# Stores of x moved to GpSimd, loads of a batch spread over its steps, first transposes a step later

## The chip, the cores and the metric

The kernel runs on one core of one Trainium2 chip. The metric is the device time of one execution in microseconds (us). The engines are named as in the profile: PE (TensorE) does matmuls and transposes, DVE (VectorE), ACT (ScalarE) and POOL (GpSimd) work on tiles, and SP (SyncE) issues most of the transfers; POOL and ACT can issue transfers of their own. Each engine works through its own instructions in order and waits on semaphores of the others.

## What is computed

Windowed attention, then a mixture of experts that takes one expert for each token, then a dense layer with softplus. All in float32, with 4 batches, 8 heads, 576 positions and 64 features to a head, so 2304 tokens of 512 features.

```python
def _attn_ref(q, k, v):                      # (4, 8, 576, 64) each
    rel = pos[:, None] - pos[None, :]
    mask_plain = (rel >= 0) & (rel < 32)                        # heads 0 to 3
    mask_dil = (rel >= 0) & (rel < 128) & (rel % 4 == 0)        # heads 4 to 7
    scores = np.where(masks, scale * (q @ k.T), -1e9)
    attn = np.exp(scores - scores.max(-1)); attn /= attn.sum(-1) + 1e-09
    return attn @ v
def _moe_ref(x, w_gate, w_output_gate, w1, w2):                 # x: (2304, 512), 8 experts
    e_idx = argmax(x @ w_gate)
    out[mask] = gate_w * eom[:, e] * (relu(x[mask] @ w1[e]) @ w2[e])
def _moe2_ref(x, w_in, w_out):               # (512, 2048), (2048, 512)
    h = x @ w_in
    return (np.maximum(h, 0.0) + np.log1p(np.exp(-np.abs(h)))) @ w_out
```

## The kernel before

Attention works on 20 tiles, five to a batch; tiles w = 0 to 3 of a batch hold 128 positions, tile w = 4 holds 64. Heads 0 to 3 (the "first half") use the plain window, heads 4 to 7 (the "second half") the dilated one. The main loop runs over steps i = 0 to 21 and is pipelined over tiles: step i computes the scores and the softmax's start of tile i (`scores` L346, L359; `softmax`, L373, L374; `exps` L382), transposes the probabilities of tile i - 1, multiplies them with v and normalises (`transpose_p` L388, `evict_p` L397, `sums` L423 to L427, `values` L415, `normalise` L437), and transposes x of tile i - 2 for the router (`transpose_x` L454, L465). A step is written out in that order, and each engine keeps it.

q and k come from DRAM as tiles `raw` (L261, `load_qk`; six buffers in rotation, each half of a batch needs two) and must be transposed before use: `transpose_qk` (L306, L314) makes one unit on PE, whose result `pqk` is evicted into `qT` and `kT` by ACT (L286, L290) or DVE (L288). A batch has ten units. They are done during the steps of the batch before; how many in each of its five steps is a small table, `QK_AT` for the later batches and `QK_0` for batch 1, whose transposes run in steps 0 to 4. v comes into `vP` (first half, L270, four transfers to a batch) and `vD` (second half, L275 and L279, two transfers to each of four heads), each kept twice, for even and odd batches. The unused parts of these tiles are cleared by POOL (`fills`, L235 to L243).

`normalise` writes the result x of a tile (five buffers) and stores it to `x_dram` through SP: the first 256 columns in one transfer (L444), the other 256 in four (L447), because the rows of the dilated half lie in another order in the tile. `x_dram` is read by the experts' gathers (L806), on POOL, through a list of tokens that POOL scatters into `idx_dram` (L600), one indirect transfer to a tile, in groups of tiles (0 to 3, 4 to 7, 8 to 10, 11 to 13, 14 to 16, 17 to 19).

All transfers of SP stand in one queue in the order in which the program writes them, and a transfer that waits holds all behind it. Beside the wait for its data or its buffer, each waits for the transfer eight places before it (eight lanes). POOL's transfers have eight lanes of their own. The expert stage and the last layer follow and are not touched.

Of the kernel before, what the change touches and what calls it, by code (L numbers as in the profile page):

```python
# [14 lines left out]
I32 = mybir.dt.int32  # L15
# [6 lines left out]
P = 128  # L22
# [18 lines left out]
def attn_moe_softplus_kernel(ctx: ExitStack, tc: tile.TileContext, q, k, v, w_gate, w_ogate, w1, w2, w_in, w_out, out, dbg=None):  # L41
    nc = tc.nc
    B, H, S, D = q.shape
# [6 lines left out]
    NW = 5  # L50
    NTL = B * NW
# [3 lines left out]
    G_PICK, G_DRAM = 2, 3  # L55
    GROUPS = [(0, 4), (4, 8), (8, 11), (11, 14), (14, 17), (17, 20)]

    const = ctx.enter_context(tc.tile_pool(name="const", bufs=1))
    dram = ctx.enter_context(tc.tile_pool(name="dram", bufs=1, space=DRAM))

    x_dram = dram.tile([NT, DM], F32, name="x_dram")
# [17 lines left out]
    first = const.tile([P, NE], F32, name="first")  # L79
    e0nt = const.tile([P, 1], F32, name="e0nt")  # L80
    tabp = const.tile([1, 1], I32, name="tabp")

    tl = {}

# [36 lines left out]
    def consts2():  # L121
        nc.gpsimd.memset(upper, 1.0)
        nc.gpsimd.affine_select(upper, upper, [[1, P]], ALU.is_gt, 0.0, base=0, channel_multiplier=-1)
        nc.gpsimd.memset(ones, 1.0)
        nc.gpsimd.memset(lg, 0.0)
        nc.gpsimd.memset(cumb, 0.0)
        nc.gpsimd.iota(rev, [[-1, NE]], base=NE, channel_multiplier=0, allow_small_or_imprecise_dtypes=True)
        nc.gpsimd.iota(eidx, [[1, NE]], base=0, channel_multiplier=0, allow_small_or_imprecise_dtypes=True)

        nc.gpsimd.memset(ebase, 0.0)  # L130
        nc.gpsimd.tensor_scalar(ebase[0:1], eidx[0:1], float(NT), None, ALU.mult)
        for b in range(B):
            nc.gpsimd.iota(pair[:, NW * b : NW * b + NW, 0], [[P, NW]], base=b * S, channel_multiplier=1)
# [121 lines left out]
    def load_qk(b, half):  # L255

        for ti, t in enumerate((q, k)):
            r = raw_p.tile([P, 2, 9 * D], F32, tag="raw", name=f"raw{b}{half}{ti}")
            raw[b, half, ti] = r
            src = t[b, 4 * half : 4 * half + 4].rearrange("(y x) (p j) d -> (x p) y (j d)", x=2, j=9)  # L260
            nc.sync.dma_start(r, src)  # L261

    def load_v(b, half):
        i = b % 2
        for h in range(4):
            h2, hp = h // 2, h % 2
            r = slice(64 * h2, 64 * h2 + 64)
            s = v[b, 4 * half + h]
            if half == 0:
                nc.sync.dma_start(  # L270
                    vP[i][r, hp, :, h2],
                    bass.AP(s.tensor, s.offset, [[D, 64], [32 * D, 17], [1, D]]),
                )
            else:
                nc.sync.dma_start(  # L275
                    vD[i][r, hp, 0:3, h2],
                    bass.AP(s.tensor, s.offset, [[4 * D, 64], [32 * 4 * D, 3], [1, 4 * D]]),
                )
                nc.sync.dma_start(  # L279
                    vD[i][64 * h2 : 64 * h2 + 48, hp, 3, h2],  # L280
                    s[4 * 96 :].rearrange("(m r) d -> m (r d)", r=4),
                )
# [44 lines left out]
    def pump(times=None):  # L327
        for e in bg[: PUMP[1]]:
            if e[1] > 0:
                e[1] -= 1  # L330
                continue
            for _ in range(PUMP[0] if times is None else times):
                e[1] = next(e[0], None)
                if e[1] is None:
                    bg.remove(e)
                if e[1] != 0:
                    break
# [81 lines left out]
    def sums(b, w):  # L419
# [7 lines left out]
        nc.vector.reciprocal(rc.rearrange("q a h c -> q a c h"), sm.rearrange("q (a c) h -> q a c h", a=2))  # L427
        pump()

    def normalise(b, w):  # L430
        d = tl[b, w]
        x = at_p.tile([P, 2, 4, D], F32, tag="x", name=f"x{b}{w}", bufs=5)
        d["x"] = x
        x2 = x.rearrange("q a h d -> q (a h d)")
        t0 = b * S + P * w
        nt = P if w < 4 else 64
        nc.vector.tensor_tensor(  # L437
            x,
            d["o"].rearrange("q a h c e -> q a (h c) e"),
            d["rc"].rearrange("q a h c -> q a (h c)").unsqueeze(3).to_broadcast([P, 2, 4, D]),  # L440
            ALU.mult,
        )
        pump()
        nc.sync.dma_start(x_dram[t0 : t0 + nt, :256], x2[:nt, :256])  # L444
        rows = x_dram[t0 : t0 + nt, 256:].rearrange("(m r) d -> m r d", r=4)
        for r in range(4):
            nc.sync.dma_start(rows[:, r], x2[32 * r : 32 * r + nt // 4, 256:])  # L447

    def transpose_x(b, w):
        d = tl[b, w]  # L450
# [557 lines left out]
    def hi_(r, j):  # L1008
        piece_hi(r, j)
# [24 lines left out]
    n = len(tiles)  # L1034
    todo, routes = [], []

    def some_qk(k):
        for _ in range(k):
            if todo:
                transpose_qk(*todo.pop(0))  # L1040

    QK_AT = [2, 2, 2, 2, 2]
    QK_0 = [0, 1, 3, 3, 3]

    EV = {}

# [21 lines left out]
    def events(i, s):  # L1068
        for what, *a in EV.get((i, s), ()):
            if what == "r":  # L1070
                bg.append([group(*a), 0, *a])
            elif what == "pl":
                logits_of(*a)
            elif what == "h":
                hi_(0, *a)
            elif what == "q":
                lo_(0, *a)
            elif what == "sc":
                diag_gathered(*a)
            elif what == "az":  # L1080
                acc0(*a)
            elif what == "mg":
                mm_gathered(a)
            elif what == "ll":
                load_late(*a)
            elif what == "go":

                e = next((e for e in bg if e[2] == a[0]), None)
                for _ in range(a[1]):
                    if e in bg:  # L1090
                        e[1] = next(e[0], None)
                        if e[1] is None:
                            bg.remove(e)
            elif what == "sl":
                g = next(g for g, (t0, t1) in enumerate(GROUPS) if t0 <= a[0] < t1)
                while any(e[2] == g for e in bg):
                    pump()
                sel_late(*a)
                split_late(*a)

    for i in range(n + 2):
        nqk = 0
        PUMP[0], PUMP[1] = (2, 1) if i < 12 else (4, 2) if i < n else (2, 2)
        if i == n - 5:
            rawx.close()
            K["wr"] = rctx.enter_context(tc.tile_pool(name="wr", bufs=RB, side="right"))
        if i == n - 4:
            per0x.close()
            K["w1"] = rctx.enter_context(tc.tile_pool(name="w1", bufs=4, side="right"))
            pctx = ExitStack()  # L1110
            for nm, bufs in (("xge", 4), ("sp0", 4), ("xl0", 5), ("sel", 4), ("rt2", 2)):
                K[nm] = pctx.enter_context(tc.tile_pool(name=nm, bufs=bufs, side="right"))
            K["slots"] = K["sel"].tile([P, CAPS[0]], F32, name="slots", bufs=1)
            nc.gpsimd.iota(K["slots"], [[1, CAPS[0]]], base=0, channel_multiplier=0, allow_small_or_imprecise_dtypes=True)
        if i < n:
            b, w = tiles[i]
            if b + 1 < B:
                nqk = (QK_AT if b else QK_0)[w]
                if w == 0:
                    if b == 0:  # L1120
                        fills(1)
                    todo += [(b + 1, *u_) for u_ in QK_UNITS]
                if w == 2:
                    for half in range(2):
                        load_v(b + 1, half)
                if w in (1, 3) and b + 2 < B:
                    load_qk(b + 2, w // 2)
            scores(b, w)
            softmax(b, w)
        if 1 <= i < n + 1:  # L1130
            transpose_p(*tiles[i - 1])
            evict_p(*tiles[i - 1])
        events(i, 0)
        some_qk(nqk - 1)
        if i < n:
            exps(*tiles[i])
        if 2 <= i:
            transpose_x(*tiles[i - 2])
            evict_x(i - 2)
            pump()  # L1140
        events(i, 1)
        if 1 <= i < n + 1:
            sums(*tiles[i - 1])
        events(i, 2)
        some_qk(min(nqk, 1))
        if 1 <= i < n + 1:
            values(*tiles[i - 1])
            normalise(*tiles[i - 1])
        events(i, 3)
        pump()  # L1150
        events(i, 4)
        pump()
        if i == n - 4:
            nc.vector.tensor_scalar(K["slots"], K["slots"], e0nt, None, ALU.add)
            K["rt"] = K["rt2"]
# [68 lines left out]
    x2, last_rank = {}, {}  # L1224
# [41 lines left out]
    for r in range(NE):  # L1266
        n = CAPS[r]
# [7 lines left out]
        for u in range(16):  # L1275
# [16 lines left out]
            if r + 1 < NE:  # L1292
                m = CAPS[r + 1]
# [6 lines left out]
            if r < NE - 1 or u < 8:  # L1300
                k_ = (r, 4 + u // 2) if u < 8 else (r + 1, (u - 8) // 2)
# [114 lines left out]
    for i in range(len(steps) + LAG):  # L1416
        if i < len(steps):
            b, f = steps[i]
# [52 lines left out]
```

## Time and profile before

| | us |
|---|---|
| median of 3 runs | 831.95 (831.78 to 834.63) |
| the profiled execution | 839.03 |
| its span in the profile | 837.5 |
| PE busy | 784.0 |
| DVE busy | 551.9 |
| ACT busy | 473.7 |
| POOL busy | 199.7 |

The granted clock of PE was 0.981 of full speed over the span. The page of the profile gives the totals, the span in 40 slices and the costliest lines. For a change inside attention three further views are of use: the waits, by engine, with the line that waits, who released it, the total, how often and the longest; the timeline, with the idle time before an instruction and its releaser in brackets; and the busy time of all engines in chosen stretches, with the granted clock and the DMA share. Times count from the start of the span.

### The profile page before, as it was taken

To read this page: it belongs to the slowest core of one execution; us is meant where nothing else is said; L and a number is where in the kernel's file an instruction comes from. 1 tells how busy PE (TensorE), PEld (TensorE's weight loads), DVE (VectorE), ACT (ScalarE), POOL (GpSimd) and SP (SyncE) were. 2 spreads that over 40 slices of the span, in tenths; PEclk is the share of its full clock that TensorE was granted. 3 is DMA by queue.
4 is the path that set the end of the run, shared out by engine and by line. 5 is a ranking of instruction groups with operands and counts; after the bars stand their busy time and mean duration, and the time that the engine had idled before them with its cause. 6 is when DMAs were issued, how large, how long until landed. Compare 5 with 4: busy or idle time off the path is not lost.

```text
span 837.5 us, 14769 instructions
## 1 busy us (share of the span) xinstructions
PE 784.0 (94%) x5542; PEld 701.9 (84%) x5543; DVE 551.9 (66%) x1079; ACT 473.7 (57%) x912; POOL 199.7 (24%) x173
## 2 busy tenths in 40 slices
PE   6788877799999999999899999999999999999995
PEld 5566645599999999999898878899999999999994
DVE  5467757474366776743778989886656665666653
ACT  3575633354546556655667566665655655655553
POOL 9501032435242454543202121211001001001001
PEclk9899989899999999999999999999999999999998
DMA  9979755418779889777832222221001001001000
GB/s 205 260 172 173 140 142 157 132 27 251 229 240 282 291 267 299 229 221 210 273 107 66 87 81 64 76 76 38 20 1 38 1 1 38 1 0 39 1 1 38
DMA packets 88844, 104.17 MB, mean 124 GB/s; under 512 B 31004, under 2 KB 65180, under 8 KB 88768
## 3 DMA queue, kind: packets, MB, share of 16 engines
q1 hardware_dynamic: 78688, 87.50, 38.3%
q0 software_dynamic: 3888, 10.12, 3.6%
q10 hardware_dynamic: 6192, 5.56, 2.0%
q8 instruction: 45, 0.74, 0.4%
q14 instruction: 31, 0.25, 0.1%
HBM read 83.98 MB, written 19.32 MB: 123 GB/s over the span
## 4 chain that ended last, share of the span: by engine, by line
PE 46%; issue 16%; DVE 6%; ACT 3%; POOL 1%; DMA 1%; SPq 0%; POOLq 0%; DVEq 0%
PE q L1380 4%; PE pg L840 4%; PE pg L841 4%; PE pg L839 4%; PE q L1378 4%; PE q L1379 4%; PE ph L839 3%; PE ph L841 3%; PE ph L840 3%; PE py L839 3%; PE py L840 3%; PE py L841 3%; DVE l L1358 1%; DVE gl L701 1%; ACT gh L1364 1%
## 5 line engine op out<-in xcount | busy, mean ns | idle before, releaser
L701 POOL TENSOR_TENSOR wl<-wr,wh 128x1024 fp32r<-128x1024 f32 (+1 forms) x46 | 99.5, 2170 | 204.0 <-ACT wh L785 108.3
L840 PE MATMUL pg<-xlm,wh 128*128 128x384 f32 x384 | 129.6, 338 | 0.0
L839 PE MATMUL pg<-xhm,wh 128*128 128x384 f32 x384 | 129.4, 337 | 0.0
L841 PE MATMUL pg<-xhm,wl 128*128 128x384 f32 x384 | 129.4, 337 | 0.0
L1380 PE MATMUL q<-wh,gl 128*128 128x512 f32 x288 | 114.0, 396 | 2.2 <-DVE gl L701 2.1
L1378 PE MATMUL q<-wh,gh 128*128 128x512 f32 x288 | 113.9, 396 | 0.4
L1379 PE MATMUL q<-wl,gh 128*128 128x512 f32 x288 | 113.1, 393 | 0.0
L1364 ACT CAST gh<-l 128x384 fp32r<-128x384 f32 x96 | 49.2, 512 | 99.9 <-DVE l L1358 99.9
L756 ACT CAST wh<-wr 128x1024 fp32r<-128x1024 f32 x72 | 75.2, 1049 | 16.2 <-ACT y L862 7.3
L701 DVE TENSOR_TENSOR gl<-l,gh 128x384 fp32r<-128x384 f32 x96 | 57.1, 595 | 41.0 <-ACT gh L1364 38.1
L839 PE MATMUL ph<-xh,wh 128*128 128x424 f32 (+7 forms) x256 | 80.7, 315 | 3.1 <-DVE hl L853 2.4
L1387 POOL DMA_INDIRECT out_dram<-o,perm_sb x18 | 18.6, 1035 | 271.9 <-DVE o L251 137.5
L839 PE MATMUL py<-hh,wh 128*128 128x424 f32 (+7 forms) x256 | 81.8, 320 | 0.0
L840 PE MATMUL py<-hl,wh 128*128 128x424 f32 (+7 forms) x256 | 80.7, 315 | 0.8 <-DVE hl L853 0.8
L841 PE MATMUL py<-hh,wl 128*128 128x424 f32 (+7 forms) x256 | 80.5, 314 | 0.0
L841 PE MATMUL ph<-xh,wl 128*128 128x424 f32 (+7 forms) x256 | 80.3, 314 | 0.0
L840 PE MATMUL ph<-xl,wh 128*128 128x424 f32 (+7 forms) x256 | 80.2, 313 | 0.0
L839 PEld LDWEIGHTS pg<-xhm,wh 128*128 128x128 f32 x384 | 72.1, 188 | 3.9
L701 DVE TENSOR_TENSOR wl<-wr,wh 128x1024 fp32r<-128x1024 f32 x42 | 61.9, 1478 | 20.4 <-ACT wh L756 14.1
L840 PEld LDWEIGHTS pg<-xlm,wh 128*128 128x128 f32 x384 | 72.1, 188 | 3.9
L841 PEld LDWEIGHTS pg<-xhm,wl 128*128 128x128 f32 x384 | 72.1, 188 | 0.0
L1349 DVE TENSOR_SCALAR w<-u 128x384 f32<-128x384 f32 x96 | 34.7, 362 | 56.4 <-ACT u L1347 55.6
(193 smaller groups left out, 1656.0 us busy)
## 6 DMA issues: line engine op xcount, KB each, us to landing
wr<-in_moe_w_dram SPq DMA_DIRECT2D x64, 512.0 KB
raw<-in_q_dram SPq DMA_DIRECT2D x8, 576.0 KB
raw<-in_k_dram SPq DMA_DIRECT2D x8, 576.0 KB
x2r<-yT_dram SPq DMA_DIRECT2D x12, 384.0 KB
vP<-in_v_dram SPq DMA_DIRECT2D x16, 272.0 KB
praw<-in_moe_w_in_dram SPq DMA_DIRECT2D x8, 512.0 KB
praw<-in_moe_w_out_dram SPq DMA_DIRECT2D x8, 512.0 KB
wr<-in_moe_w_in_dram SPq DMA_DIRECT2D x8, 512.0 KB
```

The costliest lines, as they stand in the source:

```text
L701: e.tensor_tensor(lo, src, hi.bitcast(F32), ALU.subtract)
L756: (eng or nc.scalar.copy)(d[1], d[0])
L839: nc.tensor.matmul(ps, wh, xh, start=(first and i == 0), stop=False)
L840: nc.tensor.matmul(ps, wh, xl, start=False, stop=False)
L841: nc.tensor.matmul(ps, wl, xh, start=False, stop=(last and i == k - 1))
L1349: nc.vector.tensor_scalar(w_, u, 1.0, None, ALU.add)
L1358: nc.vector.tensor_tensor(l, l, u, ALU.subtract)
L1364: nc.scalar.copy(gT[b, f][0], l)
L1378: nc.tensor.matmul(acc[b, t], gh[:, ts_], wh, start=(f == 0), stop=False)
L1379: nc.tensor.matmul(acc[b, t], gh[:, ts_], wl, start=False, stop=False)
L1380: nc.tensor.matmul(acc[b, t], gl[:, ts_], wh, start=False, stop=(f == NF - 1))
L1387: sc = nc.gpsimd.indirect_dma_start(out=out, out_offset=IndirectOffsetOnAxis(ap=perm_sb[:, b * (BT // P) + t, 0:1], axis=0), in_=o, in_off ...
```

## The change

Three things change, all in attention. x of tiles 0 to 13 (the first four routing groups) is stored by POOL: the first 256 columns directly, the other 256 by one indirect store with a table of row numbers, `xrow`, which four iotas fill at the start. Tiles w = 4 (numbers 4 and 9 among these) keep four small stores of their second half on SP. Tiles 14 to 19 keep the old way. The stores are declared independent of each other. Second, the loads for the next batches are emitted at the end of a step, behind `normalise`, and v of the next batch is split over steps w = 0, 2 and 4. Third, `QK_0` puts the first unit of batch 1 one step later.

```diff
+    xrow = const.tile([P, NTL], I32, name="xrow")
...
+        for r in range(4):
+            nc.gpsimd.iota(
+                xrow[32 * r : 32 * r + 32].rearrange("p (b w) -> p b w", w=NW),
+                [[2 * S, B], [2 * P, NW]], base=2 * r + 1, channel_multiplier=8,
+            )
...
-    def load_v(b, half):
+    def load_v(b, half, heads=range(4)):
         i = b % 2
-        for h in range(4):
+        for h in heads:
...
+    X_POOL = GROUPS[G_DRAM][1]
...
     def normalise(b, w):
...
-        nc.sync.dma_start(x_dram[t0 : t0 + nt, :256], x2[:nt, :256])
-        rows = x_dram[t0 : t0 + nt, 256:].rearrange("(m r) d -> m r d", r=4)
-        for r in range(4):
-            nc.sync.dma_start(rows[:, r], x2[32 * r : 32 * r + nt // 4, 256:])
+        i = NW * b + w
+        eng = nc.gpsimd if i < X_POOL else nc.sync
+        sts = [eng.dma_start(x_dram[t0 : t0 + nt, :256], x2[:nt, :256])]
+        if i < X_POOL and w < NW - 1:
+
+            sts.append(
+                nc.gpsimd.indirect_dma_start(
+                    out=x_dram.rearrange("t (h d) -> (t h) d", h=2),
+                    out_offset=IndirectOffsetOnAxis(ap=xrow[:, i : i + 1], axis=0),
+                    in_=x2[:, 256:],
+                    in_offset=None,
+                )
+            )
+        else:
+            rows = x_dram[t0 : t0 + nt, 256:].rearrange("(m r) d -> m r d", r=4)
+            for r in range(4):
+                sts.append(nc.sync.dma_start(rows[:, r], x2[32 * r : 32 * r + nt // 4, 256:]))
...
-    QK_0 = [0, 1, 3, 3, 3]
+    QK_0 = [0, 0, 3, 3, 4]
...
-                if w == 2:
-                    for half in range(2):
-                        load_v(b + 1, half)
-                if w in (1, 3) and b + 2 < B:
-                    load_qk(b + 2, w // 2)
             scores(b, w)
             softmax(b, w)
...
             values(*tiles[i - 1])
             normalise(*tiles[i - 1])
+        if i < n and b + 1 < B:
+
+            for half, heads in (((0, (0, 1)),), (), ((0, (2, 3)), (1, (0,))), (), ((1, (1, 2, 3)),))[w]:
+                load_v(b + 1, half, heads)
+            if w in (1, 3) and b + 2 < B:
+                load_qk(b + 2, w // 2)
```

On PE, at the border of steps 1 and 2, the order before is this (`pp` are the transposes of p of tiles 0 and 1, `pqk` units of batch 1, `o` the values of tile 0, `s` the scores of tile 2, `px` the transposes of x of tile 0):

```order
L388 MATMUL pp_382<-identf,p_352 128x128 x4
L306 MATMUL pqk_395<-identf,raw_231 128x128 x4
L415 MATMUL o_402<-vP_118,pt_387 32x2x64 x8
L415 MATMUL o_402<-vD_120,pt_387 32x2x64 x8
L346 LDWEIGHTS identb
L346 MATMUL s_438<-mask_w,identb 128x512
L359 MATMUL s_438<-kT_116,qT_114 32x128 x16
L388 MATMUL pp_460<-identf,p_379 128x128 x4
L306 MATMUL pqk_467<-identf,raw_233 128x128 x4
```

and after:

```order
L394 MATMUL pp_385<-identf,p_357 128x128 x4
L421 MATMUL o_398<-vP_119,pt_390 32x2x64 x8
L421 MATMUL o_398<-vD_121,pt_390 32x2x64 x8
L352 LDWEIGHTS identb
L352 MATMUL s_423<-mask_w,identb 128x512
L365 MATMUL s_423<-kT_117,qT_115 32x128 x16
L394 MATMUL pp_445<-identf,p_382 128x128 x4
L312 MATMUL pqk_452<-identf,raw_232 128x128 x4
L312 MATMUL pqk_459<-identf,raw_234 128x128 x4
```

The unit that stood ahead of the values of tile 0 now stands behind the scores of tile 2.

On SP, the queue behind q and k of batch 1 before (`raw` q and k of batch 2 first, `x` of tiles 0 to 2, `vP` and `vD` of batch 1):

```order
L261 DMA raw_358<-in_k_dram 128x2x576
L444 DMA x_dram<-x_419 128x256
L447 DMA x_dram<-x_419 32x256 x4
L270 DMA vP_119<-in_v_dram 64x17x64 x4
L275 DMA vD_121<-in_v_dram 64x3x256
...
L279 DMA vD_121<-in_v_dram 48x256
L444 DMA x_dram<-x_518 128x256
L447 DMA x_dram<-x_518 32x256 x4
L261 DMA raw_525<-in_q_dram 128x2x576
L261 DMA raw_527<-in_k_dram 128x2x576
L444 DMA x_dram<-x_608 128x256
```

and after, from the last transfer of q and k of batch 1 on (`raw_419` to `raw_596` are q and k of batch 2):

```order
L267 DMA raw_327<-in_k_dram 128x2x576
L276 DMA vP_120<-in_v_dram 64x17x64 x2
L267 DMA raw_419<-in_q_dram 128x2x576
L267 DMA raw_421<-in_k_dram 128x2x576
L276 DMA vP_120<-in_v_dram 64x17x64 x2
L281 DMA vD_122<-in_v_dram 64x3x256
L285 DMA vD_122<-in_v_dram 48x256
L267 DMA raw_594<-in_q_dram 128x2x576
L267 DMA raw_596<-in_k_dram 128x2x576
L281 DMA vD_122<-in_v_dram 64x3x256
...
L470 DMA x_dram<-x_766 16x256 x4
L276 DMA vP_119<-in_v_dram 64x17x64 x2
```

The stores of x are gone from it up to the small ones of tile 4 (`x_766`), and three heads of `vD` stand behind the second pair of q and k of batch 2.

On POOL, from the last memset of the start on, the order before and then after (`idx_dram` is the routing scatter of tiles 0 to 3):

```order
L242 MEMSET vP_119 64x34x64
L243 MEMSET vD_121 64x8x256
L600 DMA idx_dram<-pair,rposi_932 18944x2 x4
L600 DMA idx_dram<-pair,rposi_1371 18944x2 x4
L600 DMA idx_dram<-pair,rposi_1568 18944x2 x3
```

```order
L249 MEMSET vD_122 64x8x256
L456 DMA x_dram<-x_415 128x256
L460 DMA x_dram<-x_415,xrow 4608x256
L456 DMA x_dram<-x_503 128x256
L460 DMA x_dram<-x_503,xrow 4608x256
...
L460 DMA x_dram<-x_1052,xrow 4608x256
L629 DMA idx_dram<-pair,rposi_912 18944x2 x4
L456 DMA x_dram<-x_1154 128x256
L460 DMA x_dram<-x_1154,xrow 4608x256
L456 DMA x_dram<-x_1257 64x256
```

The stores of x stand one pair to a tile between the memsets and the scatters, which keep their place among the tiles.

## Rows read from the trace of the kernel before

**Rows 1.** Page, part 1: busy us, share of the span, instructions.
```profile
PE 784.0 (94%) x5542; PEld 701.9 (84%) x5543; DVE 551.9 (66%) x1079; ACT 473.7 (57%) x912; POOL 199.7 (24%) x173
```
**Rows 2.** Waits in 15:215, PE, then DVE: total, times, longest, in us.
```profile
PE pqk L306 <- DMA raw<-in_q_dram: 5.2, 1, 5.2
PE s L359 <- issue: 4.8, 6, 1.1
...
DVE x L437 <- remote: 15.2, 4, 4.9
```
**Rows 3.** Timeline of PE: start, us, line, operation, count, idle before and releaser.
```profile
27.40 1.09 PE L306 MATMUL pqk<-identf,raw 128*128 128x128 f32 x4 [5.21 <-DMA raw<-in_q_dram]
28.42 1.08 PE L415 MATMUL o<-vP,pt 128*32 128x128 f32 x16
29.28 1.08 PE L415 MATMUL o<-vD,pt 128*32 128x128 f32 x16
30.29 0.57 PE L346 MATMUL s<-mask_w,identb 128*128 128x512 bf16 x1
...
48.68 1.14 PE L359 MATMUL s<-kT,qT 128*32 128x128 f32 x16 [1.77 <-ACT kT L286]
...
58.26 0.65 PE L415 MATMUL o<-vP,pt 128*32 128x128 f32 x16
```
**Rows 4.** Timeline of ACT, steps 1 to 4.
```profile
28.53 1.38 ACT L290 ACTIVATE qT<-pqk 64x512 f32<-64x512 f32 x2 [5.19 <-PE pqk L306]
32.98 0.59 ACT L397 COPY pt<-pp 128x512 f32<-128x512 f32 x1 [3.06 <-PE pp L388]
...
48.24 0.38 ACT L286 COPY kT<-pqk 64x128 f32<-64x128 f32 x1 [0.46 <-DVE qT L288]
```
**Rows 5.** Stretches: us, busy and count by engine, PE clock, DMA share, GB/s.
```profile
25.00:30.00 5.00, 2.60 (x36) 2.12 (x36) 0.00 (x0) 1.37 (x2) 4.89 (x4) 0.50 1.03 377
...
35.00:40.00 5.00, 4.74 (x78) 3.33 (x67) 3.07 (x5) 4.88 (x9) 0.00 (x0) 1.00 1.22 182
...
100.00:105.00 5.00, 4.25 (x82) 3.24 (x82) 4.45 (x23) 2.11 (x6) 0.00 (x0) 1.00 1.36 164
```
**Rows 6.** Page, part 6 and the DMA view: issues, KB each.
```profile
raw<-in_q_dram SPq DMA_DIRECT2D x8, 576.0 KB
...
vD<-in_v_dram SPq DMA_DIRECT2D x16, 192.0 KB
```
**Rows 7.** Waits of SP's queue in 15:215.
```profile
SPq L444 <- DVE x L437: 10.9, 4, 5.3
```
**Rows 8.** Timeline of SP's queue, v of batch 1.
```profile
33.40 4.08 SPq L270 DMA_DIRECT2D vP<-in_v_dram  x4
```
**Rows 9.** Timeline of POOL: memset, scatters, the direct issue, gathers.
```profile
30.66 1.80 POOL L243 MEMSET vD<- 64x2048 f32 x1
74.94 1.17 POOL L600 DMA_INDIRECT idx_dram<-pair,rposi  x1 [42.48 <-DVE rc L427]
...
113.07 0.96 POOL L600 DMA_INDIRECT idx_dram<-pair,rposi  x1 [0.30 <-issue]
...
133.54 0.96 POOL L600 DMA_INDIRECT idx_dram<-pair,rposi  x1 [0.30 <-issue]
140.84 0.83 POOL L708 DMA_DIRECT2D idx<-idx_dram  x1 [6.34 <-DMA x_dram<-x]
144.41 1.45 POOL L806 DMA_INDIRECT xg<-x_dram,idx  x1 [2.74 <-DMA x_dram<-x]
...
271.69 1.00 POOL L806 DMA_INDIRECT xg<-x_dram,idx  x1 [5.91 <-DMA idx<-idx_dram]
```
**Rows 10.** Timelines of DVE and ACT near POOL's indirect transfers.
```profile
115.76 0.69 DVE L437 TENSOR_TENSOR x<-o,rc 128x512 f32<-128x512 f32 x1 [4.93 <-remote]
...
135.49 0.58 ACT L397 COPY pt<-pp 128x512 f32<-128x512 f32 x1 [4.33 <-remote]
...
273.62 0.45 ACT L862 COPY y<-py 128x344 f32<-128x344 f32 x1 [0.99 <-issue]
```

More of the change, by code (lines that the diff above doesn't have):

```diff
@@ L428, in sums @@
         pump()
+    X_POOL = GROUPS[G_DRAM][1]
+    x_stores = []
     def normalise(b, w):
@@ L443, in normalise @@
         pump()
-        nc.sync.dma_start(x_dram[t0 : t0 + nt, :256], x2[:nt, :256])
-        rows = x_dram[t0 : t0 + nt, 256:].rearrange("(m r) d -> m r d", r=4)
-        for r in range(4):
-            nc.sync.dma_start(rows[:, r], x2[32 * r : 32 * r + nt // 4, 256:])
+        i = NW * b + w
[14 more added lines that the diff above has]
+                sts.append(nc.sync.dma_start(rows[:, r], x2[32 * r : 32 * r + nt // 4, 256:]))
+        for k_, st in enumerate(sts):
+            on_pool = i < X_POOL and (k_ == 0 or w < NW - 1)
+            for e, e_pool in x_stores:
+                if on_pool or e_pool:
+                    tc.declare_no_dep(st.ins, e.ins, reason="no two stores of x have a row and half in common")
+            x_stores.append((st, on_pool))
     def transpose_x(b, w):
```

## The prediction

> **What bounds the kernel now.** I read the profile's totals first: TensorE is busy 784.0 us of the span [rows 1]. The rest of the kernel is the same code in the same order, and the expert stage that follows attention is matmul after matmul, so I take a shift of the end of attention to reach the end of the kernel one to one. Everything that the change touches lies in attention. There I read the waits of TensorE: the longest is 5.2 us, for q of batch 1; beside it stand 4.8 us in six waits that no row explains ("issue") [rows 2]. The timeline then shows where the long wait stands: the first transposes of batch 1 (27.40) are queued ahead of the values of tile 0 (28.42), which need none of that data [rows 3]. After it ACT limits: from 32.98, its first copy of step 2, to 48.24, its last key copy of step 4 [rows 4], it runs with small gaps, and TensorE stands 1.77 us behind that chain before the matmul at 48.68 [rows 3]. The busy time in stretches says the same: in 35:40 ACT has 4.88 and TensorE 4.74 of 5 us [rows 5].
>
> **Part one: the first transposes one step later.** It removes no work; one unit (four transposes and their two evictions) goes from step 1 to step 2, and step 4 has four units instead of three. The values of tile 0 then wait only for the last of v of batch 0. That landing has no row. It is bounded: the transfer is queued just ahead of q of batch 1, which landed at about 27.4, and a q transfer holds 576 KB, at 377 GB/s (the stretch 25:30) 1.6 us [rows 3, 5, 6]. So v is there at about 25.8. The half of the values that reads it (the second, 0.86 us behind 28.42) can start at about 25.9 instead of 29.28, and step 2 at about 27.0 instead of 30.29 [rows 3]: 3.3 us earlier. If the landings overlapped, the ends are 2 us and the whole 5.2 us.
>
> Of this, steps 2 to 4 give part back. ACT has to do one more pair of evictions inside its full chain: 1.38 us, which lay in the hole of step 1 before [rows 4]. TensorE gets four more transposes there, 1.09 us at the clock of 27.40 and less at a higher one [rows 3]. ACT is the later one: the chain starts 3.3 us earlier and is 1.4 us longer, so its last key copy and the matmul behind it come 1.9 us earlier. The granted clock was 0.50 in 25:30, the lower of its two levels (1.2 and 2.4 GHz), around the idle wait [rows 5]; if the shorter wait leaves it higher, the values get shorter, but ACT still sets the end, so I count nothing. Ends: 1.3 us if step 4 with its four units adds a small wait, 3.3 us if ACT's gaps absorb the pair. **Term: -1.9 us.**
>
> **Part two: x on GpSimd's queue, and the loads.** SP loses 62 issues. What it waited for DVE's x is 10.9 us in four waits [rows 7]; without them the queue reaches the loads of v of batch 1, now at 33.40 [rows 8], right behind q and k of batch 1 and runs ahead as far as buffers and its eight lanes allow. That is worth nothing by itself, since TensorE's long wait for a load is the one of part one [rows 2]. The three v heads that are now emitted last stand behind a q and a k transfer on SP, and those wait until the transposes of batch 1's first half free a buffer (step 3, some 38 us by step 2 and the steps' length of about 5). From there 2 x 576 KB and 3 x 192 KB and their small rests, about 1.9 MB, take 10.5 us at 182 GB/s: about 49 [rows 5, 6]. The values that need them start at 58.26, or 56.4 after the shift [rows 3]. Zero, with some 7 us of cover; without it, each us late is a us of TensorE.
>
> GpSimd gets four more iotas among its memsets and 26 stores behind the last of them, which ends at 32.46. A direct store is priced by the only direct issue there, 0.83 us, an indirect one by 0.96 us and the 0.30 of gap that stands behind such an issue: 14 x 0.83 + 12 x 1.26 = 26.7 us, spread over the 75 us from 32 to 107, where the queue has only the scatters of the first group and the start of the second [rows 9]. Engine work it has none there, so nobody waits; the routing scatter that now has a store or two ahead of it has its reader only at 144.41 [rows 9]. DVE's x has five buffers, five steps or some 25 us, until its store must have landed. Zero for GpSimd as an occupant; what the stores may do to other engines is the first rival.
>
> **Sum.** -1.9 + 0 + 0. The profiled execution takes 839.03 us (span 837.5) and would take 837.1; it lies 7.1 us above the median of the runs, 831.95, and I carry that difference over: **830.0 us**.
>
> One rule speaks against part two. The trace shows GpSimd's indirect issue at 1.17 us at 74.94 and at 0.96 us at 113.07 and 133.54, with DVE at work in between [rows 9]. The Trainium skill, "SBUF — State Buffer", in its box on the "DVE blocks DMA" trap, says that a DMA issued from GpSimd needs descriptors which GpSimd writes through a port that DVE can lock, and that a hardware queue avoids this. These rows show no such stretching, and with some 25 us of cover for a store the sum is 830.0 by the row and by the rule.
>
> **Rival 1, slower: the stores hold up the other engines.** After the first tiles, the stalls that have "remote" or "issue" as releaser lie where GpSimd's indirect DMAs run or have just ended. DVE's x has 15.2 us of "remote" in four waits [rows 2]. Behind the seven scatters of which the last is at 113.07, TensorE gets score matmuls one by one (the 4.8 us of "issue") and DVE's x stands 4.93 us; behind the three whose last is at 133.54, ACT stands 4.33 [rows 2, 9, 10]. 4.8 over seven is 0.7 us for each DMA, 4.33 over three 1.4. If each of the 12 indirect stores costs that, the time is 830.0 + 8.4 to 16.8 = 838 to 847. It passes the bound for slower (below) when one store costs over 0.5 us. Against it: in the expert stage such DMAs run from 271.69 and ACT goes on at 273.62 with 0.99 us of idle [rows 9, 10]; the scatters write single pairs of words, the stores whole rows of 1 KB; two stores in a step are no burst; and the 7.1 us that only the profiled execution has could be the sum of these holds, which then are the profiler's.
>
> **Rival 2, faster: the holds belong to the loads.** The DMA share is 1.36 in 100:105, right ahead of the longest hold, and there SP brought v of batch 3 in one go [rows 5]. If that backlog is the cause, the earlier and spread loads of the new order take away the 4.93 us [rows 10]: 830.0 - 4.9 = 825.1. Against it: 35:40 has 1.22, and TensorE is full [rows 5]. Nearly the same time, 826.7, comes if part one keeps the whole 5.2 us.
>
> **Rival 3: part one does not do what it says.** The values of tile 0 then wait for v about as long as the transposes did for q, or ACT eats the whole gain: 832.
>
> **How the numbers follow.** About 0.5%, 4.2 us, is what a measurement of this kernel tells from no change: faster is below 827.8, slower above 836.1. Forecast (830.0, its own range 828.6 to 831.2) 0.42; rival 3, 0.10; rival 2 with the whole 5.2 us, 0.24; rival 1, 0.24. Rival 2 lies below 827.8, rival 1 above 836.1 but for its mildest cases, and a few per cent of the forecast fall below. So faster 0.25, within 0.5% 0.52, slower 0.23. The range takes in rival 2 (824) and the lower third of rival 1 (841), which leaves out some 0.15 to 0.2.
>
> **What the profile after would show.** Right: TensorE goes from the transposes of p at about 21.5 to the values of tile 0 with a wait of some 4 us, on v or on nothing named; step 2 starts near 27; the score matmul of step 5 that stood at 48.68 stands near 46.8; SP has no wait for DVE's x in batches 0 and 1 but at their fifth tile; GpSimd issues pairs of stores from 32 on, and no engine has a new long wait. Wrong: step 2 not before 29 (rival 3); new "remote" or "issue" waits on several engines within a us or two of a store of x, and steps of 8 us where they were 5 to 6 (rival 1); or the hold that ends at 115.76 gone (rival 2). A wait of the values of tile 5 for v would show the cover of the loads wrong.

## The result: 822.9 us, 1.2% faster

| | before | after |
|---|---|---|
| median, us (20 runs each) | 832.45 | 822.9 |
| ratio | | 0.988 (0.9858 to 0.9903) |
| profiled execution, us | 839.03 | 821.58 |
| its span | 837.5 | 820.0 |

The forecast was 830.0 with a range from 824.0 to 841.0 and "no change" as the likeliest. The gain is 9.5 us, five times the term of 1.9 us. The page of the kernel after, totals:

```profile
span 820.0 us, 14730 instructions
...
PE 776.2 (95%) x5542; PEld 697.9 (85%) x5543; DVE 552.0 (67%) x1079; ACT 474.0 (58%) x912; POOL 220.2 (27%) x203
```

PE has the same 5542 matmuls as in [rows 1]; POOL is busy 20.5 us longer with its 30 new instructions. The start of the kernel after, timeline of PE (columns as in [rows 3]):

```profile
21.91 0.73 PE L394 MATMUL pp<-identf,p 128*128 128x128 f32 x4
23.36 0.65 PE L421 MATMUL o<-vP,pt 128*32 128x128 f32 x16 [0.72 <-issue]
23.80 0.43 PE L421 MATMUL o<-vD,pt 128*32 128x128 f32 x8
24.45 0.43 PE L421 MATMUL o<-vD,pt 128*32 128x128 f32 x8 [0.22 <-DMA vD<-in_v_dram]
24.80 0.39 PE L352 MATMUL s<-mask_w,identb 128*128 128x512 bf16 x1
...
43.75 1.13 PE L365 MATMUL s<-kT,qT 128*32 128x128 f32 x16 [1.45 <-ACT kT L292]
```

The values of tile 0 stand right behind the transposes of p. Their wait for v is 0.22 us, the last of v being there at 24.45, and step 2 begins at 24.80, where [rows 3] had 30.29. The matmul behind ACT's last key copy stands at 43.75 instead of 48.68. POOL in the kernel after, at the first stores, in step 10, and at the gathers (columns as in [rows 9]):

```profile
33.28 0.81 POOL L456 DMA_DIRECT2D x_dram<-x  x1
34.39 1.04 POOL L460 DMA_INDIRECT x_dram<-x,xrow  x1 [0.30 <-issue]
...
73.99 0.96 POOL L629 DMA_INDIRECT idx_dram<-pair,rposi  x1 [0.30 <-DMA x_dram<-x]
74.95 0.57 POOL L456 DMA_DIRECT2D x_dram<-x  x1
75.83 0.98 POOL L460 DMA_INDIRECT x_dram<-x,xrow  x1 [0.30 <-issue]
...
132.05 0.99 POOL L835 DMA_INDIRECT xg<-x_dram,idx  x1 [2.57 <-DMA idx<-idx_dram]
```

The 12 indirect stores take 0.96 to 1.04 us each and the 14 direct ones 0.56 to 0.81, so the price of POOL's own time (0.96 and 0.83 in [rows 9]) was nearly right for the first and high for the second. The first gather comes at 132.05 instead of 144.41.

A first trap lies in the two traces themselves. They differ by 17.5 us, the medians by 9.5. Steps can be counted off at the mask matmul that opens each (L346 before, L352 after); these are lengths in us, from its rows:

| step | before | after |
|---|---|---|
| 1 | 11.03 | 5.34 |
| 4 | 4.71 | 5.84 |
| 5 | 8.61 | 8.28 |
| 6 to 9 | 4.88, 4.79, 5.16, 4.44 | 4.88, 4.80, 5.15, 4.45 |
| 10 | 9.63 | 7.52 |
| 11 | 6.01 | 4.84 |
| 15 | 12.47 | 8.20 |
| 18 | 9.06 | 5.65 |

Steps 1 to 5 are the new transposes. Steps 10, 15 and 18 are those in which POOL issues its routing scatters; in the trace before they hold all engines for 2 to 4 us [rows 10], in the trace after they do not, although POOL's bursts there are longer. Whether the change took the holds away, or the two executions differ by something else, is what the experiments had to tell first.

### The profile page after: what moved, and what is told of

The parts are those of the page before. It is cut to its first block, busy times and chain, and to the rows that moved or that the text cites. A ratio compares the mean times of both kernels' runs of the same rounds, so it can differ in the third digit from the quotient of the medians.

```text
span 820.0 us, 14730 instructions
## 1 busy us (share of the span) xinstructions
PE 776.2 (95%) x5542; PEld 697.9 (85%) x5543; DVE 552.0 (67%) x1079; ACT 474.0 (58%) x912; POOL 220.2 (27%) x203
## 4 chain that ended last, share of the span: by engine, by line
PE 52%; issue 9%; DVE 8%; ACT 4%; POOL 1%; DMA 1%; SPq 0%; POOLq 0%; DVEq 0%
PE pg L869 5%; PE pg L870 5%; PE q L1410 5%; PE pg L868 5%; PE q L1409 5%; PE q L1408 5%; PE ph L868 3%; PE ph L870 3%; PE py L868 3%; PE ph L869 3%; PE py L869 3%; PE py L870 3%; DVE l L1388 2%; ACT gh L1394 1%; DVE l L1386 1%
```

## The experiments

Each group below was run together on one chip, with runs of the kernel before between, and the ratios are against those. The groups ran on several chips.

**First group: the parts alone.** Later first transposes alone:

```diff
-    QK_0 = [0, 1, 3, 3, 3]
+    QK_0 = [0, 0, 3, 3, 4]
```

> The kernel before with the later first transposes alone. If part one is worth what the trace after shows at step 6 (49.61 instead of 54.55), the time is 832.4 - 4.9 = 827.5, and step 2 starts near 25 in its trace. If only the 1.9 us of the forecast come from it, 830.5. If the start needs SP's free queue as well (v lands later because of x's stores), it stays at 832.

Measured: 826.67 us, ratio 0.9974 (0.995 to 0.9997). Step 2 starts at 25.48 and step 6 at 50.17, some 4 us earlier. The medians differ by 3.5 us, and by its interval the ratio is worth 0.2 to 4.2.

Stores alone (the hunk of `normalise` in the diff and the table `xrow`, loads and `QK_0` as before):

```diff
-        nc.sync.dma_start(x_dram[t0 : t0 + nt, :256], x2[:nt, :256])
+        eng = nc.gpsimd if i < X_POOL else nc.sync
+        sts = [eng.dma_start(x_dram[t0 : t0 + nt, :256], x2[:nt, :256])]
```

> The kernel before with the stores of x on GpSimd alone, loads and transposes in the old places. If the holds of all engines in attention come from SP's stores of x beside GpSimd's scatters, they go here and the time falls by some 4.5 us to 828. If they belong to the loads of v, they stay: 832. If the stores themselves cost, 838 and more (0.7 us for each of 12).

Measured: 824.2 us, ratio 0.9926 (0.9895 to 0.9956). This part, at zero in the forecast, is the larger one.

Loads alone (the loads behind `normalise`, v split over steps w = 0, 2 and 4):

```diff
+            for half, heads in (((0, (0, 1)),), (), ((0, (2, 3)), (1, (0,))), (), ((1, (1, 2, 3)),))[w]:
+                load_v(b + 1, half, heads)
```

> The kernel before with the loads at the end of a step and v spread over steps, stores on SP and transposes as before. If the backlog of v causes the holds, the time falls by some 4.5 us to 828 and the hold behind the second group's scatters is gone. If the stores of x cause them, or both are needed, it stays near 832; SP then still stands behind DVE's x, so the loads come no earlier, and 833 to 836 is possible where a load comes late.

Measured: 833.49 us, ratio 1.0032 (1.0009 to 1.0055): slower. And loads with the later transposes, x on SP:

> The change without its stores: loads and transposes as after, x on SP. If the parts add up and the stores are worth nothing, 823; if the stores carry the second half of the gain, 827.5, with holds of several us behind the scatters; if loads without stores come late, 828 to 832.

Measured: 833.86 us, ratio 1.0046 (1.002 to 1.0073). The waits of PE in 15:215 of this kernel, its timeline, and SP's queue at the same place say why:

```profile
PE o L415 <- DMA vD<-in_v_dram: 12.5, 7, 5.3
```

```profile
83.98 0.65 PE L415 MATMUL o<-vP,pt 128*32 128x128 f32 x16
89.90 0.66 PE L415 MATMUL o<-vD,pt 128*32 128x128 f32 x8 [5.27 <-DMA vD<-in_v_dram]
92.47 0.65 PE L415 MATMUL o<-vD,pt 128*32 128x128 f32 x8 [1.91 <-DMA vD<-in_v_dram]
```

```profile
77.11 0.42 SPq L444 DMA_DIRECT2D x_dram<-x  x1
79.30 2.22 SPq L447 DMA_DIRECT2D x_dram<-x  x4
81.56 0.73 SPq L275 DMA_DIRECT2D vD<-in_v_dram  x1
...
89.68 0.59 SPq L279 DMA_DIRECT2D vD<-in_v_dram  x1
```

With x on SP's queue the last heads of v stand behind the stores of two tiles and a pair of q and k. They are issued from 81.56 to 89.68, and PE waits for them from 84.63 on. It is not DVE that holds SP here (0.5 us in 70:96): from 77.5 to 88.7 SP waits four times for an earlier transfer, a store of x or q and k, each time the one eight places before, 7.2 us in all. The spread loads are no gain; they need a queue without the stores of x. With the stores on POOL none of these waits is among those of PE.

In all four traces step 15 takes 7.56 to 8.28 us, and none has a hold, with stores on SP or on POOL. So neither SP's stores nor the burst of v are enough for the holds of [rows 10].

**Second group: the other pairs, and the kernel before again.** Later transposes with stores, and stores with loads:

> The change without its loads: first transposes later, x stored by GpSimd, loads in the old places. If the spread loads are worth nothing beside free stores, this is the whole gain, 0.988 of before; if they earn something of their own (v of a batch not in one go), it stays at 0.992 to 0.994.

> The change with the old table of first transposes. If the later transposes are worth the 4 to 5 us by which step 6 starts earlier, this is at 0.993 to 0.994 of before; if the stores alone give the gain and the start is made up later, 0.988; if the wait for q of batch 1 shrinks by itself once x is off SP, between.

Measured: 839.06 us, ratio 1.0027 (1.0001 to 1.0053), and 843.48 us, ratio 1.0064 (1.0039 to 1.0088). Both slower than before, where the first group makes one expect about 0.990 and 0.996. The kernel before, twice:

> The kernel before once more, for its trace. If the holds of several us behind GpSimd's scatters (steps 10, 15 and 18 of 9.6, 12.5 and 9.1 us) belong to every execution, they stand here too; if they come by chance, some of these steps take the 7.3, 7.6 and 5.6 us that the kernel with only the later transposes had, and the time is lower by as much.

> The same a second time: the steps that hold in all three traces of the kernel before are its own, the others chance. By chance alone the time lies between 823 and 838 as the steps add up.

Measured: 840.12 and 837.34 us. Steps 10, 15 and 18 take 9.30, 12.52 and 8.97 us in the one, 8.50, 12.20 and 8.65 in the other: in this group every trace has the holds. With the stores, step 10 takes 11.79 and 12.11 us and step 15 14.56 and 15.06.

**Third group: the parts where the holds are.**

> The kernel before on this chip, for its trace. Two chips so far differ: on one, kernels with x on SP showed no hold behind GpSimd's scatters (step 15 of 7.6 us), on the other it was 12.2 to 12.5 us in each. If the hold belongs to the chip, step 15 here is near one of the two, and every kernel of this call agrees with it.

> The kernel after. If the holds belong to the chip and GpSimd's stores lengthen a burst of scatters there, it is 0.988 of before on a chip without holds and 1.00 to 1.005 on a chip with them (the 4 to 5 us of the start against 4 to 6 us of longer holds). If the gain does not hang on the chip, 0.988 here too.

> Stores of x on GpSimd alone. Chip without holds: 0.993 as before, and its trace beside that of before on the same chip shows where the 6 us were. Chip with holds: 1.00 to 1.007, with step 10 near 12 us and step 15 near 14.6 us.

> Later first transposes alone. The start is not a matter of the holds, so on any chip step 6 comes some 4 us earlier and the time is 0.995.

Measured: before 836.28 us, with steps 10 and 15 of 8.83 and 12.92, so again holds. The kernel after 838.84 us, ratio 1.0019 (0.9993 to 1.0044); stores alone 1.0074 (1.004 to 1.0108); transposes alone 0.9953 (0.9929 to 0.9977). So the same change is worth 1.2% without the holds and nothing that can be told with them, and it is the stores whose sign turns. The kernel after in step 10 with holds, POOL, then ACT, DVE and PE:

```profile
73.70 0.96 POOL L629 DMA_INDIRECT idx_dram<-pair,rposi  x1 [0.30 <-issue]
74.66 0.57 POOL L456 DMA_DIRECT2D x_dram<-x  x1
75.53 0.98 POOL L460 DMA_INDIRECT x_dram<-x,xrow  x1 [0.30 <-issue]
```

```profile
77.21 0.59 ACT L403 COPY pt<-pp 128x512 f32<-128x512 f32 x1 [6.00 <-PE px L483]
```

```profile
77.10 0.29 DVE L520 COPY lt<-pl 128x128 f32<-128x128 f32 x1 [3.00 <-PE px L483]
```

```profile
73.35 0.60 PE L394 MATMUL pp<-identf,p 128*128 128x128 f32 x4
73.79 0.84 PE L312 MATMUL pqk<-identf,raw 128*128 128x128 f32 x4
74.47 0.27 PE L483 MATMUL px<-identf,x 128*128 128x128 f32 x1
75.51 0.49 PE L483 MATMUL px<-identf,x 128*128 128x128 f32 x3 [0.77 <-issue]
77.81 0.83 PE L312 MATMUL pqk<-identf,raw 128*128 128x128 f32 x4 [1.81 <-PE px L483]
```

The same ACT copy in the kernel after without holds, where the transposes `pp` stand at 73.50, PE and then ACT:

```profile
73.50 0.66 PE L394 MATMUL pp<-identf,p 128*128 128x128 f32 x4
74.25 0.59 ACT L403 COPY pt<-pp 128x512 f32<-128x512 f32 x1 [2.74 <-PE pp L394]
```

ACT's copy needs the transposes `pp`, done by 74. It starts 0.75 us behind their start in the trace without holds and at 77.21 in the other, 0.7 us after POOL's last transfer of the burst ends (75.53 + 0.98). DVE and PE go on within the same us. In steps 6 to 9, where POOL issues one pair, the steps take 4.89, 4.78, 5.17 and 4.45 us with holds too: a pair alone costs nothing, a pair at the end of a burst does.

**Fourth group: the burst.** Scatters of the first three groups spread over the steps (`late_scat` holds them; `normalise` takes one out, from step 15 on up to three):

```diff
-        nc.vector.tensor_copy(posi, places[g])
+        if g <= G_PICK:
+            late_scat.extend((g, posi, w) for w in range(t1 - t0))
+            return
...
+        for _ in range(min(len(late_scat), 1 if i < 14 else 3)):
+            g_, posi_, w_ = late_scat.pop(0)
+            nc.vector.tensor_copy(posi_[:, w_ : w_ + 1], places[g_][:, w_ : w_ + 1])
+            scatter_one(g_, posi_, w_)
```

> The kernel before, for its trace on this chip: steps 10, 15 and 18 near 9, 12.5 and 9 us on a chip with holds, near 7.3, 7.6 and 5.6 us on one without.

> The kernel after with the routing scatters of the first three groups spread, one to a step up to step 15 and three to a step behind it, instead of bursts of four and seven. If a burst makes the hold, step 10 takes about 7.5 us and step 15 about 8.2 us on a chip with holds, and the time there falls by 6 to 10 us against the kernel after, to 0.99 of before. If each indirect DMA holds the engines by its own length, the holds move to the steps that now have them and the time stays at 1.00. On a chip without holds: 0.988, as after.

The first group's scatters a second time, into a table of their own (`for dst in (idx_dram, idx_two) if g == 0 else (idx_dram,)`):

> The kernel after with the four scatters of the first group done a second time into a table that nobody reads, so that GpSimd's burst in step 10 has nine indirect DMAs. If the hold grows with the burst, step 10 takes 5 us more than in the kernel after (about 17 us on a chip with holds). On a chip without holds 7.5 us as before, or some 10 if a long enough burst holds there too.

The second half of x by four direct stores on POOL:

```diff
-                nc.gpsimd.indirect_dma_start(
+            e2_ = nc.gpsimd if i < X_POOL and w < NW - 1 else nc.sync
+            sts.append(e2_.dma_start(rows[:, r], x2[32 * r : 32 * r + nt // 4, 256:]))
```

> The kernel after with the second half of x stored by four direct DMAs of GpSimd instead of one indirect one. GpSimd then issues five DMAs for each tile, about 4.5 us a step. If any burst of GpSimd's DMAs holds the engines, every step from 3 to 14 grows by 2 us or more on a chip with holds; if only indirect ones do, steps 5 to 9 stay at 8.3, 4.9, 4.8, 5.2 and 4.5 us and step 10 falls below 11.8.

Measured: before 834.04 us with steps 10, 15 and 18 of 7.33, 8.26 and 5.61: no holds, and yet this is the chip of the third group. The holds belong neither to the kernel nor to the chip. Spread scatters 825.15 us, ratio 0.992 (0.9891 to 0.995), no better than after; double scatters 824.55 us, step 10 of 7.52; direct stores 826.02 us, step 10 of 7.34 (the last two are one execution each). So a burst of nine indirect transfers does not hold the engines by its length alone, and no difference between direct and indirect stores can be told. What spreading, doubling or direct stores would do where holds are was not seen.

This group gave what was missing, a trace of the kernel before without holds, and with it the place of the stores' gain. Its attention up to step 19 is 4.35 us behind the kernel after (128.33 against 123.98), all of it from the start. Then it falls back further. The kernel before without holds: PE at the gathers' products and at the first expert matmul, then POOL at the first gather, the waits of ACT in 120:215, and SP's queue:

```profile
146.31 0.80 PE L912 MATMUL xacc<-diag,xg 128*128 128x128 f32 x2 [1.69 <-DMA xg<-x_dram,idx]
148.49 1.37 PE L912 MATMUL xacc<-diag,xg 128*128 128x128 f32 x4 [1.38 <-DMA xg<-x_dram,idx]
...
165.74 0.43 PE L839 MATMUL ph<-xh,wh 128*128 128x424 f32 x1 [0.22 <-issue]
```

```profile
138.48 1.01 POOL L806 DMA_INDIRECT xg<-x_dram,idx  x1 [3.66 <-DMA x_dram<-x]
```

```profile
ACT xl L943 <- DMA xl<-x_dram: 11.4, 3, 4.0
```

```profile
121.89 2.85 SPq L743 DMA_DIRECT2D wr<-in_moe_w_dram  x5
124.84 0.56 SPq L444 DMA_DIRECT2D x_dram<-x  x1
125.45 3.41 SPq L447 DMA_DIRECT2D x_dram<-x  x4
...
139.70 0.48 SPq L932 DMA_DIRECT2D xl<-x_dram  x1
```

And the kernel after, first expert matmul and SP's queue:

```profile
155.24 0.43 PE L868 MATMUL ph<-xh,wh 128*128 128x424 f32 x1 [0.46 <-issue]
```

```profile
107.04 5.06 SPq L772 DMA_DIRECT2D wr<-in_moe_w_dram  x5
112.20 0.88 SPq L456 DMA_DIRECT2D x_dram<-x  x1
...
128.65 0.48 SPq L961 DMA_DIRECT2D xl<-x_dram  x1
```

Before, the five loads of the first expert's weights stand at the end of a late queue (121.89) and the stores of the tiles behind them; the gather waits for a store of x, its data come while `xl` and more weights are loaded too, and PE waits 3.1 us for them (in two waits) and ACT 11.4 us for `xl`. After, the weights start at 107.04, and PE waits for no transfer there. From step 19 to the first expert matmul it is 37.4 us before and 31.3 after. Kernels with the stores on POOL and without holds have 31.0 to 32.4 (stores alone 31.0, direct 32.3), and the kernel with the later transposes alone, stores on SP, 34.0. So in these traces the stores save 3 to 6 us at the hand-over from attention to the experts. The stores alone show nothing else: they reach step 19 at 129.64, 1.3 us behind before, and the first expert matmul at 160.60, 5.1 us ahead.

How late SP's queue is can be read at one place. DVE picks the first expert's number (`tabp`), and SP cannot issue these weights without it. Its cast, before and then after, and behind it SP's wait for it in 90:215 of the kernel after:

```profile
110.15 0.14 DVE L646 CAST tabp<-pk 1x1 int32<-1x1 f32 x1
105.83 0.14 DVE L675 CAST tabp<-pk 1x1 int32<-1x1 f32 x1
SPq L647 <- DVE tabp L675: 13.8, 1, 13.8
```

Before, the weights are issued 11.7 us after the number is there (transposes alone 11.1). After, it is 1.2 us, SP having waited 13.8 us for it; the other four traces without holds and with these stores on POOL have 1.2 as well. It is not DVE's x that makes the queue late. In 60:122 of before SP waits 1.4 us for DVE and 9.7 for earlier transfers, and the stores themselves fill it: the rows of their 70 transfers add up to 42.4 of the 91.5 us from 30 to 121.5.

Two things limit this reading. Loads alone and loads with transposes have x on SP and still the shortest hand-overs, 30.7 and 30.5 us, with 0 and 0.6 us of ACT's waits for `xl`: they reach step 19 some 7 and 9 us later than before, SP has partly caught up (6.5 and 6.6 us behind the number), and what they save here they have lost in the waits for v. So it is the late queue that costs, and the stores on POOL are one way out. And part of the 37.4 us is the clock. In 148.30:153.30 of before, right behind its waits, the granted clock was 0.55 with PE busy 4.81 of 5 us. An estimate from windows of 1 us: the hand-over has 13.7 us at the lower level before and 6.8 after, PE is busy in 11 and 6 of them, and half of that is lost, which makes 2.5 of the 6 us.

**Fifth group: which stores.** Both with the later transposes and the loads in the old places; stores of tiles 9 to 13 alone on POOL, and of tiles 0 to 8 alone (`X_POOL = 9`):

> Later first transposes, and of the stores only those of tiles 9 to 13 on GpSimd. If the lag at the end of SP's queue is what the stores remove, this has nearly the whole gain without holds, 0.988 to 0.990 of before, with 31 to 32.5 us from step 19 to the first expert matmul; if the lag comes from the first tiles, 0.995 to 0.997 as with the transposes alone (34 us). With holds: 1.00, since the bursts of steps 10 and 15 are as long as after.

> Later first transposes, and of the stores only those of tiles 0 to 8 on GpSimd. If the late tiles carry the gain, 0.995 to 0.997 and 34 us or more from step 19 to the first expert matmul; if the first ones do, 0.988 to 0.990. With holds: these stores stand alone between the bursts, so 0.995, as with the transposes alone, and steps 10 and 15 stay at 9 and 12.5 us.

Measured: 834.73 us, ratio 0.9955 (0.9931 to 0.9979), and 835.15 us, ratio 0.9969 (0.9945 to 0.9993). Both traces have holds, so the question of the hand-over stays unanswered: late tiles or all of them. With holds there is little to win at it: in every one of the eleven traces with holds SP issues the first weights 1.2 to 2.8 us after the expert's number, with x on SP too, and the hand-over takes 31.8 to 39.8 us without an order between the two kinds. For the late tiles 1.00 was expected with holds, which the interval leaves out.

What the two tell is how a hold grows. With the four scatters alone step 10 takes 8.50 to 9.63 us (the five traces with holds that have all of x on SP). With the pair of tile 8 behind the scatters (early tiles) it takes 12.28, like the kernel after (11.84). The late tiles have no store in that burst (tile 9's starts at 80.43, behind the step), and yet step 10 takes 10.88. The late tiles' last scatter, ACT and PE, then ACT and PE with the early tiles, then the same in the second group's first trace of before:

```profile
73.56 0.96 POOL L630 DMA_INDIRECT idx_dram<-pair,rposi  x1 [0.30 <-issue]
75.81 0.59 ACT L403 COPY pt<-pp 128x512 f32<-128x512 f32 x1 [4.98 <-PE pp L394]
77.43 1.08 PE L421 MATMUL o<-vP,pt 128*32 128x128 f32 x16
```

```profile
75.75 0.59 ACT L403 COPY pt<-pp 128x512 f32<-128x512 f32 x1 [6.16 <-PE px L483]
77.37 1.08 PE L421 MATMUL o<-vP,pt 128*32 128x128 f32 x16
```

```profile
80.52 0.58 ACT L397 COPY pt<-pp 128x512 f32<-128x512 f32 x1 [4.72 <-PE px L454]
81.68 0.65 PE L415 MATMUL o<-vP,pt 128*32 128x128 f32 x16
```

ACT stands 4.7 to 5.6 us behind the scatters alone and 6.0 to 6.2 with the pair, so the pair itself adds about 1 us. Most of the rest is the clock: the values behind the hold take 1.08 us for each half instead of 0.65, at a granted clock of 0.50 (77.40:79.30 with the late tiles, 77.30:79.20 with the early ones) against 1.00 (81.60:82.70 of before). In step 15 the seven scatters give 12.12 with the early tiles, near the 12.20 to 12.92 of kernels with x on SP, and 14.02 with the late ones, which add stores there. My expectation for the early tiles, step 10 at 9 us, was wrong, since tile 8's pair falls into that burst.

| group | holds | before, us | ratios |
|---|---|---|---|
| first | no | 830.19 | transposes 0.9974, stores 0.9926, loads 1.0032, transposes and loads 1.0046 |
| second | yes | 836.44 | transposes and stores 1.0027, stores and loads 1.0064 |
| third | yes | 837.73 | transposes 0.9953, stores 1.0074, after 1.0019 |
| fourth | no | 832.48 | after with spread scatters 0.992 |
| fifth | yes | 838.60 | transposes and late stores 0.9955, transposes and early stores 0.9969 |

The median of before alone tells the two kinds apart: 830 to 832.5 without, 836 to 839 with holds. The comparison of the result has 832.45 and fits the first kind; the profiled execution of before (839.03) shows the second.

No version beats both kernels under both conditions. Without holds none is clearly better than the kernel after; with them the later transposes alone (0.9953) and with the late stores (0.9955) are the fastest measured.

## Why the prediction was wrong

**Part one, right in its mechanism, too small.** The values of tile 0 move ahead of the wait, step 2 starts earlier, ACT's chain gives part back: all of this stands in the trace. Two terms were off. The landing of v was put at 25.8 by letting the transfer of q follow it whole; it is 24.45, so step 2 gains 5.5 us between the two traces, not 3.3; 1.3 of the difference is the landing, the rest the values behind it, short at a granted clock of 1.00 (24:29) where before had 0.50. And ACT's chain gives back 1.1 us (step 4: 5.84 for 4.71) and step 5 returns 0.3, so step 6 starts 4.9 us earlier (49.61 for 54.55), with 1.9 forecast. Alone, the part is worth 0.26% and 0.47% by its ratios, 2 to 4 us (the medians differ by 3.5 and 3.7); the start varies between executions (step 6 of before from 52.88 to 54.55).

**Part two, the step that failed: "zero".** The loads of v were costed well: beside stores on POOL they are in time, and the cost of loads that come late was real, 7 to 12.5 us of PE's waits, where x stayed on SP. But the argument priced SP by its wait for DVE (10.9 us, [rows 7], of which 4.9 lie behind 125 us, in stores that stay on SP) and held that an unblocked SP is worth nothing because PE has no wait on a later load [rows 2]. It left out that the 62 issues fill the queue by themselves, and it followed the loads close behind the stores and not the end of the queue, almost 90 us later: the weights of the first expert, the stores of the last tiles and the reloads of x. The trace it was read from has holds, and there the queue is hardly late at its end (weights at 120.58, the number at 118.71), so this trace could not show the loss; the order of the queue could. I had the reader of `x_dram` in hand (the gather at 144.41 in [rows 9], which waits 2.74 us for a store of x) and used it only as cover for POOL's stores. Without holds the hand-over is shorter by 3 to 6 us, some of it clock, and the stores alone measure 0.74%.

**Rival 1 was the right mechanism in the wrong place.** With POOL's stores steps 10 and 15 take 1.6 to 3.3 us longer where holds occur (third group), about 1 us of it in step 10 the hold and most of the rest the clock behind it, and the stores alone cost 0.74% there. That the longer steps are all of this cost is not shown: in its trace the hand-over is 7.9 us longer too, with PE busy throughout 161.90:176.90 at a granted clock of 0.54. It was priced as 0.7 to 1.4 us for each of 12 stores; measured, only steps in which stores fall into a burst of scatters grow, those with a pair alone do not. Its time of 838 to 847 is met by the kernels with stores in the second and third groups (838.8 to 843.6), though before itself is at 836 to 838 there, so the loss is smaller than forecast. The comparison of the result had no holds.

**Rival 2 named nearly the right time (825.1) for a wrong reason.** The holds are not caused by the backlog of v: the kernels with spread loads have them in the second and third groups, and kernels with v in one go lack them in the first and fourth.

**The remark on the 7.1 us.** That the profiled execution's excess over the median might be the sum of the holds was right in size: groups with holds are 4 to 8 us slower in the kernel before. But it is not a matter of one profiled execution: whole groups of runs have them, and others do not. The profiled time and the median were of two kinds, and I used one to carry the other.

**The rule on GpSimd's transfers.** The prediction cites the Trainium skill, "SBUF — State Buffer", for it. The trace after agrees with the row and not with a stretching: its indirect stores take 0.96 to 1.04 us with DVE at work. The holds are no case of it either, since in them POOL goes on and PE and ACT stand with DVE.

**What stays open.** What makes a group of runs have holds, and what the engines wait for in one, no run here shows; the third and fourth groups differ in this on one chip. Whether spread scatters remove them was not seen, as that kernel met a group without, and which tiles' stores carry the gain was not seen, as the fifth group met one with them. How much of the stores' gain and cost is the clock is open too. The run's mean granted clock (median of the runs) was 0.986 with the stores alone against 0.981 before in the first group, and 0.976 against 0.981 in the third. An estimate: 0.005 of the mean is 8 us at half the clock, so up to 4 us either way. No run changed the clock alone, and whether it is a cause or only follows shorter and longer waits is not shown.

## What to carry to other kernels

An in-order transfer queue that is full pays at its far end: before a move of transfers is costed at nothing, count what the moved issues take in the queue, not only what they wait, and follow it to its last critical entry to see who waits there. A wait that is early in the queue order but whose data nobody needs yet is best removed by order alone, as with the first transposes, which gained with and without holds. And before two traces are subtracted, one should see whether a third trace of the same kernel agrees with either.

## What the runs showed of the hardware

During bursts of GpSimd's indirect transfers PE, ACT and DVE stand together in some groups of runs and not in others: step 15, with seven of them, takes 12.2 to 12.9 us or 7.6 to 8.3 in kernels with the stores on SP. Where this occurs, the engines go on soon after the last transfer of the burst ends (ACT after 0.7 to 1.9 us in step 10 of the eleven traces with holds). A pair of stores at the end of the burst keeps ACT about 1 us longer; a pair alone in a step costs nothing. The granted clock behind such a hold was 0.50 or 1.00 in step 10, which made two halves of values 1.08 us each or 0.65 and 0.62. A direct store of 128 rows of 1 KB costs GpSimd 0.57 us, an indirect one 0.98 and a gap of 0.30. Stores take time in SP's queue beside what they wait for DVE: the rows of 70 stores of 16 to 128 KB add up to 42.4 us, with 1.4 us of waits for DVE in 60:122.
